# Probabilities times values in plain fp32 over four column groups of TensorE, in an attention and MLP kernel

## The chip, the cores and the metric

The kernel runs on one core of a Trainium2 chip. The metric is the device time of one execution in microseconds (us), the median over the runs. The engines are named as in the profile: PE is TensorE's matmul, PEld its weight loads, DVE is VectorE, ACT is ScalarE, POOL is GpSimd, SP is SyncE, which only issues DMAs here.

## The reference

The input is one sequence of 2048 tokens with 1024 features, all in fp32. It is normalized, passes an attention of 32 heads with 32 features each and is added to itself; then it is normalized twice and passes an MLP with 3584 hidden features. The attention works in four segments of 512 tokens. Within a segment it is plain causal softmax attention, and a memory of the earlier segments is mixed in by a gate:

```python
for s in range(N):                                     # N = 4 segments, L = 512 tokens
    logits = jnp.einsum("bhqd,bhkd->bhqk", qs, ks) * scale + mask
    p = _softmax(logits, axis=-1)
    a_dot = jnp.einsum("bhqk,bhkd->bhqd", p, vs)       # the product that is changed
    pq = phi(qs)
    num = jnp.einsum("bhld,bhde->bhle", pq, M)
    den = jnp.einsum("bhld,bhd->bhl", pq, z)[..., None] + 1e-6
    outs.append(g * num / den + (1.0 - g) * a_dot)
    M, z = M + jnp.einsum("bhld,bhle->bhde", phi(ks), vs), z + jnp.einsum("bhld->bhd", phi(ks))
h = x + o @ wo                                         # o: the heads' outputs side by side
h2 = h + mlp(_layernorm(h))                            # normalizes once more, then w1, gelu, w2
```

## The kernel before, in words

PE multiplies rounded operands (type fp32r) in one pass over the columns. To keep fp32's precision the kernel splits an operand in an upper half (the rounded value) and a lower half (what the rounding left) and adds up products of halves; three matmuls make a projection (`mm3`, lines 116 to 118).

The kernel treats the sequence in two halves of 1024 tokens. For each half it runs the attention, then the product with wo, then the MLP. In the attention the outer loop goes over eight groups of four heads and the inner one over the half's two segments. `dense` makes the projections of one group and segment (tiles kps, qps, vps) and prepares the values; `heads` treats the four heads of the group and segment before it, and `interleave` alternates the two, so that PE always has projections between the steps of a head. At the end of a half the last heads are interleaved with the first products with wo (tile pwo).

A head is a softmax over 512 keys, in four blocks of 128 keys (`jk`), causal: block `jk` is seen by queries from `128*jk` on, so it has 512, 384, 256 or 128 query columns. `qk` makes the logits (tile pqk), DVE adds the mask and takes the maximum, ACT takes the exponential into tile pr (`soft`, line 552). `ptr` transposes the probabilities on PE into tile ppt (in PSUM, two buffers) in three portions: n = 0 is block 0, n = 1 the blocks 1 and 3, n = 2 block 2. ACT copies each portion into pth, the upper half, and DVE subtracts into ptl, the lower half (`sub`, line 600).

`av` multiplies with the values, in two steps: n = 0 for the blocks 0 and 1, n = 1 for 3 and 2. The weights are a tile vs with 64 columns for each block and head: 32 columns are the values' upper half, 32 their lower half. Each block is multiplied with pth and with ptl, and all eight matmuls add up in one PSUM tile po with 64 partitions (one buffer, tag `av`). Between them `one_small` puts small matmuls of the memory (tiles pm and pmm). Then ACT copies partitions 32 to 63 of po into the head's rows of the tile ot, and `av_out` adds partitions 0 to 31 on DVE (line 624).

The order of the steps is written out: `PLAN = ('q1 r S2', 'q0 a0', 'q2 t0 w a1', 'q3 s0 o', 't1', 's1 t2')`. A letter is a step (q: `qk`, t: `ptr`, s and S: `sub`, a: `av`, o: `av_out`, r: `inverse`, w: `weigh`), the digit its argument, and between two entries the projections go on. a, o and S belong to the head before the one that t and s treat, and that is the head before the one of q. So `av_out` of one head stands two entries before the end of its slot, and a0 of the next head, which writes the one buffer of po again, in the second entry of the next slot. A scheduler of the framework then sets the final order on each engine's queue, by its own estimates; each queue runs in order.

Of the kernel before, what the change touches and what calls it, by code (L numbers as in the profile page):

```python
# [10 lines left out]
F32 = mybir.dt.float32  # L11
F32R = mybir.dt.float32r
AF = mybir.ActivationFunctionType
ALU = mybir.AluOpType
# [3 lines left out]
P = 128  # L18
# [21 lines left out]
def raw(ap):  # L40
    return ap.bitcast(F32)


def build(tc, x, wq, wk, wv, wo, beta, w1, b1, w2, b2, out):
    nc = tc.nc
# [3 lines left out]
    psum = top.enter_context(tc.tile_pool(name="psum", bufs=1, space=PSUM))  # L49

    def ps_dense(name):
        return psum.tile([P, 512], F32, tag="d", name=name, bufs=3)
# [33 lines left out]
    acts = {}  # L86
# [258 lines left out]
    def attention(half, first):  # L345
        ab, mask = acts["ab"], acts["mask"]
# [3 lines left out]
        def tmp(name):  # L350
            return ab.tile([P, 512], F32, tag="tmp", name=name, bufs=5)
# [34 lines left out]
        def one_small():  # L386
            if small:
                small.pop(0)()
# [16 lines left out]
        def dense(g, sl, ws, u):  # L405
# [58 lines left out]
            nc.scalar.copy(vt, vps)  # L464
            vs = ab.tile([P, 16, 64], F32R, name="vs", bufs=2)
            u["vs"] = vs
            omt = u["omt"] = tmp("omt") if s > 0 else None

            def late():
                vn = ps_dense("vn")  # L470
                for c in range(4):
                    nc.tensor.transpose(vn[:, c * P:(c + 1) * P], vt[:, c * P:(c + 1) * P], ident)
                vn3 = vn.rearrange("p (a b) -> p a b", b=DH)
                nc.scalar.copy(vs[:, :, 0:32], vn3)
                nc.vector.tensor_tensor(vs[:, :, 32:64], vn3, raw(vs[:, :, 0:32]), op=ALU.subtract)
                yield
                if s > 0:
                    om = tmp("om")

                    def memory(i2, ps):  # L480
                        pm = ps.rearrange("p (a b) -> p a b", a=2)
                        rg = ab.tile([P, 2, 32], F32, name="rg", bufs=2)[:, :, 0:4]
                        nc.vector.scalar_tensor_tensor(
                            rg, pm[:, :, 128:132], DEN_EPS, bb[:, 4 * g:4 * g + 4].unsqueeze(1).to_broadcast([P, 2, 4]),
                            op0=ALU.add, op1=ALU.mult)
                        nc.vector.reciprocal(rg, rg)
                        nc.vector.tensor_tensor(
                            om[:, i2 * 256:(i2 + 1) * 256].rearrange("p (a h e) -> p a h e", a=2, h=4),
                            pm[:, :, 0:128].rearrange("p a (h e) -> p a h e", h=4),
                            rg.unsqueeze(3).to_broadcast([P, 2, 4, DH]), op=ALU.mult)  # L490

                    for i2 in range(2):
                        smalls("pm", [(lambda ps, ii=ii: ps[:, 256 * ii:256 * ii + 132],
                                       pqh[:, (2 * i2 + ii) * P:(2 * i2 + ii + 1) * P],
                                       pql[:, (2 * i2 + ii) * P:(2 * i2 + ii + 1) * P], mzh, mzl, True, True)
                                      for ii in range(2)], partial(memory, i2))
                left = len(small)
                if s < 3:
                    def update(pmm):
                        nc.vector.tensor_tensor(MZ[:, g, 0:P], pmm[:, 0:P], MZ[:, g, 0:P], op=ALU.add)  # L500
                        own = MZ[:, g, 0:P].rearrange("p (h e) -> p h e", h=4)
                        nc.gpsimd.tensor_tensor(own, own, hsel.unsqueeze(2).to_broadcast([P, 4, DH]), op=ALU.mult)
                        z = ZC[:, g:g + 1]
                        nc.gpsimd.tensor_scalar(z, z, zc, None, op0=ALU.add)
                        nc.gpsimd.tensor_scalar(MZ[:, g, 128:132], hsel, z, None, op0=ALU.mult)

                    smalls("pmm", [(lambda ps: ps[:, 0:P].rearrange("p (a b) -> p a b", a=4),
                                    pkh[:, c * P:(c + 1) * P], pkl[:, c * P:(c + 1) * P],
                                    vs[:, 4 * c:4 * c + 4, 0:32], vs[:, 4 * c:4 * c + 4, 32:64], c == 0, c == 3)
                                   for c in range(4)], update)  # L510
                total = len(small)
                while len(small) > total - left:
                    yield
                yield
                if s > 0:
                    pom = ps_dense("pom")
                    for i in range(4):
                        one_small()
                        nc.tensor.transpose(pom[:, i * P:(i + 1) * P], om[:, i * P:(i + 1) * P], ident)
                    if s == 3:  # L520
                        yield
                        while acts["pth"][0] < 2:
                            yield
                    op = nc.scalar.copy(omt, pom)
                    if s == 3:
                        tc.add_manual_dep(op.ins, acts["pth"][1].ins.name, NOSYNC, reason="program order")
                while small:
                    yield
# [5 lines left out]
        koff = [0, 512, 1024, 896]  # L534
# [45 lines left out]
        def ptr(st, n):  # L580
            grp = ((0,), (1, 3), (2,))[n]
            if n == 0:
                st["pth"] = ab.tile([P, 1280], F32R, name="pth", bufs=2)
                st["ptl"] = ab.tile([P, 1280], F32R, name="ptl", bufs=2)
            pr, pth, ptl = st["pr"], st["pth"], st["ptl"]
            ppt = psum.tile([P, 512], F32, tag="pt", name="ppt", bufs=2)
            base = koff[grp[0]]
            w = 0
            for jk in grp:
                for i in range(jk, 4):  # L590
                    one_small()
                    o = koff[jk] - base + (i - jk) * P
                    nc.tensor.transpose(ppt[:, o:o + P], pr[:, offs[i] + jk * P:offs[i] + (jk + 1) * P], ident)  # L593
                    w += P
            acts["pth"] = n, nc.scalar.copy(pth[:, base:base + w], ppt[:, :w])  # L595
            st["sub", n] = (ptl[:, base:base + w], ppt[:, :w], raw(pth[:, base:base + w]))

        def sub(st, n):
            o, x0, x1 = st["sub", n]
            nc.vector.tensor_tensor(o, x0, x1, op=ALU.subtract)  # L600

        def av(st, n):
            u, j = st["u"], st["j"]
            if n == 0:
                st["po"] = psum.tile([P, 512], F32, tag="av", name="po", bufs=1)[0:64, :]
            po = st["po"]
            for jk in (0, 1) if n == 0 else (3, 2):
                w = 512 - P * jk
                v = u["vs"][:, 4 * jk + j, :]
                for part in ("pth", "ptl"):  # L610
                    if (jk, part) != (3, "ptl"):
                        one_small()
                    nc.tensor.matmul(po[:, P * jk:], v, st[part][:, koff[jk]:koff[jk] + w],  # L613
                                     start=(jk, part) == (0, "pth"), stop=(jk, part) == (2, "ptl"))
            if n == 1:
                if j == 0:
                    u["ot"] = ab.tile([P, 512], F32, name="ot", bufs=1)
                nc.scalar.copy(u["ot"][32 * j:32 * j + 32, :], po[32:64, :])

        def av_out(st):  # L620
            u, j, po = st["u"], st["j"], st["po"]
            ot = u["ot"]
            b = slice(32 * j, 32 * j + 32)
            nc.vector.tensor_tensor(ot[b, :], po[0:32, :], ot[b, :], op=ALU.add)
            if j == 3:
                w = u["w"]
                nc.gpsimd.tensor_tensor(w, ot, w, op=ALU.mult)
                if u["omt"] is not None:
                    nc.gpsimd.tensor_tensor(w, w, u["omt"], op=ALU.add)
                if u["g"] < NG - 1:  # L630
                    nc.sync.dma_start(o_dram[u["s"]][u["g"]], w)
                else:
                    oh, ol = o_tiles(half, u["s"] % 2)
                    split(None, w, oh[:, NG - 1, :], ol[:, NG - 1, :], hi_eng="scalar", lo_eng="vector")
# [35 lines left out]
        for g in range(NG):  # L670
            for sl in range(2):
                u = {"g": g, "s": 2 * half + sl}
# [24 lines left out]
    def o_tiles(half, sl):  # L697
        if ("o", half, sl) not in acts:
            acts["o", half, sl] = seg_tiles(sl, "o")
        return acts["o", half, sl]  # L700
# [626 lines left out]
    for half in range(2):  # L1327
# [5 lines left out]
        ab = acts["ab"]  # L1333
# [132 lines left out]
```

## Time and profile before

| | |
|---|---|
| median of 3 runs | 2314.42 us (2314.29 to 2317.33) |
| span of the profiled execution, first to last instruction | 2309.1 us |
| PE busy | 2273.1 us, 98% of the span, 11801 matmuls |
| DVE, ACT, POOL busy | 1519.7, 1227.7, 830.6 us |
| L600, 384 subtractions on DVE | 227.3 us, 600 ns each |
| L613, 1024 matmuls on PE, sum of their durations | 154.1 + 156.0 us |

The profile tells for each instruction its engine, its line, the tiles it writes and reads, when it starts and how long it takes. Matmuls are pipelined: the next one starts before the last one ends, so their durations add up to more than the time they take from PE; the distance from start to start tells that. "x512" after a group counts its instructions; "idle before" is the time that the engine stood still ahead of them, with what ended it. The span was taken from one execution; the median of the runs lies 5.3 us above it.

### The profile page before, as it was taken

How to read it: one execution, taken by the hardware profiler on the slowest of the kernel's cores; microseconds unless marked ns; L12 is line 12 of the kernel's file. 1: busy time of each engine (PE TensorE's matmuls, PEld its weight loads, DVE VectorE, ACT ScalarE, POOL GpSimd, SP SyncE). 2: the span in 40 equal slices, each digit the busy share in tenths (PEclk: the TensorE clock that was granted, in tenths of full speed). 3: DMA queues.
4: the chain of work that ended last, by engine and by line, in shares of the span. 5: the costliest groups of instructions: out<-in, count | busy, mean ns of one | idle time of the engine just before them, and what ended most of it. 6: DMA issues, size and time to landing. Idle time of an engine off the chain costs nothing.

```text
span 2309.1 us, 34959 instructions
## 1 busy us (share of the span) xinstructions
PE 2273.1 (98%) x11801; PEld 1895.7 (82%) x11801; DVE 1519.7 (66%) x3045; ACT 1227.7 (53%) x2581; POOL 830.6 (36%) x686
## 2 busy tenths in 40 slices
PE   8999999999999999999999998999999999999999
PEld 6888888877888887888888886788888888888887
DVE  6777777776655565777777776574566766566663
ACT  6777777774453445777777775363344223332221
POOL 4222222224244442233232224244445654155430
PEclk9999999999999999999999999999999999999999
DMA  6333343344466654433333343466567976476772
GB/s 187 104 95 97 98 102 95 94 140 164 138 209 173 186 166 138 120 100 95 95 95 99 95 118 119 160 202 195 156 190 265 348 249 217 152 259 218 249 235 92
DMA packets 329885, 364.00 MB, mean 158 GB/s; under 512 B 28750, under 2 KB 221802, under 8 KB 329706
## 3 DMA queue, kind: packets, MB, share of 16 engines
q1 hardware_dynamic: 266538, 325.06, 46.5%
q10 hardware_dynamic: 63168, 36.71, 5.3%
q8 instruction: 93, 1.52, 0.3%
q14 instruction: 86, 0.70, 0.1%
HBM read 234.98 MB, written 76.35 MB: 135 GB/s over the span
## 4 chain that ended last, share of the span: by engine, by line
PE 69%; DMA 1%; POOL 1%; ACT 1%; DVE 1%; issue 1%; SPq 0%; POOLq 0%; ACTq 0%; DVEq 0%
PE po L1300 23%; PE bps L904 10%; PE cps L904 7%; PE dps L904 6%; PE po L613 3%; PE ppt L593 3%; PE pqk L543 2%; PE vps L116 1%; PE vps L117 1%; PE vps L118 1%; PE kps L116 1%; PE kps L117 1%; PE qps L117 1%; PE qps L116 1%; PE kps L118 1%; PE qps L118 1%
## 5 line engine op out<-in xcount | busy, mean ns | idle before, releaser
L552 ACT ACTIVATE pr<-pr,mx 128x256 f32<-128x256 f32 (+3 forms) x512 | 287.1, 561 | 163.5 <-DVE mx L544 154.7
L544 DVE CUSTOM_DVE_ANT_0 pr<-pqk,mask 128x256 f32<-128x256 f32 (+3 forms) x512 | 244.5, 486 | 107.1 <-PE pqk L543 105.9
L600 DVE TENSOR_TENSOR ptl<-ppt,pth 128x512 fp32r<-128x512 f32 (+1 forms) x384 | 227.3, 600 | 94.9 <-ACT pth L595 92.4
L593 PE MATMUL ppt<-ident,pr 128*128 128x128 f32 x1280 | 223.1, 277 | 1.0 <-DVE ptl L600 0.8
L595 ACT CAST pth<-ppt 128x512 fp32r<-128x512 f32 (+1 forms) x384 | 194.0, 517 | 40.2 <-PE ppt L593 33.1
L93 POOL TENSOR_TENSOR wl<-wr,wh 128x1024 fp32r<-128x1024 f32 x52 | 124.8, 2399 | 229.5 <-PE pqk L543 128.0
L1310 DVE TENSOR_TENSOR c<-c,po 128x512 f32<-128x512 f32 x160 | 105.4, 683 | 149.6 <-PE po L1300 146.7
L593 PEld LDWEIGHTS ppt<-ident,pr 128*128 128x128 f32 x1280 | 165.0, 141 | 30.8 <-DVE ptl L600 1.9
L543 PE MATMUL pqk<-ks,qs 96*128 96x256 f32 (+3 forms) x512 | 161.6, 316 | 0.0
L613 PE MATMUL po<-ptl,vs 128*64 128x512 f32 (+3 forms) x512 | 154.1, 310 | 4.3 <-DVE ptl L600 4.1
L613 PE MATMUL po<-pth,vs 128*64 128x512 f32 (+3 forms) x512 | 156.0, 327 | 0.0
L1300 PE MATMUL po<-w2h,zh 128*128 128x512 f32 x378 | 120.8, 389 | 0.0
L543 PEld LDWEIGHTS pqk<-ks,qs 96*128 96x128 f32 x512 | 96.5, 189 | 21.6 <-issue 0.2
L904 PE MATMUL bps<-zh,sb 128*128 128x512 f32 x336 | 111.1, 391 | 0.0
L904 PE MATMUL bps<-zh,sa 128*128 128x512 f32 x336 | 110.8, 390 | 0.0
L1157 POOL TENSOR_TENSOR w2r<-w2r 128x512 f32<-128x512 f32 x54 | 85.5, 1595 | 70.2 <-DMA w2r<-in_B_w 63.6
L116 PE MATMUL vps<-yh,wh 128*128 128x512 f32 x256 | 109.4, 427 | 0.9 <-DVE MZ L500 0.9
L116 PE MATMUL kps<-yh,wh 128*128 128x512 f32 (+1 forms) x264 | 110.0, 417 | 0.0
L116 PE MATMUL qps<-yh,wh 128*128 128x512 f32 x256 | 106.9, 418 | 0.0
L1300 PE MATMUL po<-w2h,hl 128*128 128x512 f32 x322 | 103.0, 390 | 0.0
L117 PE MATMUL kps<-yl,wh 128*128 128x512 f32 (+1 forms) x264 | 102.3, 388 | 0.1
L118 PE MATMUL kps<-yh,wl 128*128 128x512 f32 (+1 forms) x264 | 101.9, 386 | 0.0
(253 smaller groups left out, 6548.4 us busy)
## 6 DMA issues: line engine op xcount, KB each, us to landing
hr<-h_dram SPq DMA_DIRECT2D x112, 448.0 KB, 5.7
w2r<-in_B_w SPq DMA_DIRECT2D x122, 256.0 KB, 4.1
r<-in_B_w SPq DMA_DIRECT2D x56, 512.0 KB, 4.8
h_dram<-ht ACTq DMA_DIRECT2D x84, 256.0 KB, 3.8
ks<-kh SPq DMA_DIRECT2D x256, 64.0 KB, 2.0
qs<-qh SPq DMA_DIRECT2D x256, 64.0 KB, 2.0
wr<-in_A_wo SPq DMA_DIRECT2D x32, 512.0 KB, 4.5
wx<-in_B_w SPq DMA_DIRECT2D x56, 256.0 KB, 3.6
```

Of the source, the lines that this page charges most:

```text
L116: nc.tensor.matmul(ps, ah, bh, start=first, stop=False)
L117: nc.tensor.matmul(ps, ah, bl, start=False, stop=False)
L118: acts["mm"] = nc.tensor.matmul(ps, al, bh, start=False, stop=last)
L543: nc.tensor.matmul(pqk[:, :n], u["qs"][j][:, i * P:(i + 1) * P], u["ks"][j][:, 0:n], start=True, stop=True)
L544: nc.vector.tensor_tensor_reduce(out=st["pr"][:, offs[i]:offs[i] + n], in0=pqk[:, :n], in1=mask[:, 512 - n:512], op0=ALU.add, op1=ALU.min, ...
L552: nc.scalar.activation(pi, pi, AF.Exp, bias=mx[:, i:i + 1], scale=-1.0, accum_out=mx[:, 4 + i:5 + i])
L593: nc.tensor.transpose(ppt[:, o:o + P], pr[:, offs[i] + jk * P:offs[i] + (jk + 1) * P], ident)
L595: acts["pth"] = n, nc.scalar.copy(pth[:, base:base + w], ppt[:, :w])
L600: nc.vector.tensor_tensor(o, x0, x1, op=ALU.subtract)
L613: nc.tensor.matmul(po[:, P * jk:], v, st[part][:, koff[jk]:koff[jk] + w], start=(jk, part) == (0, "pth"), stop=(jk, part) == (2, "ptl"))
L904: nc.tensor.matmul(ps, x_[:, c, :], y_[:, c, :], start=first and c == 0 and n == 0, stop=last and c == 3 and n == 2, skip_group_check=True)
L1300: nc.tensor.matmul(ps, x_[:, k], y_[k], start=opens and k == 0 and i == 0, stop=closes and k == self.KP - 1 and i == 2, skip_group_check=True)
```

## The change

The probabilities are no longer split: ACT copies ppt into one tile pt in plain fp32, and the subtraction on DVE goes. `late` in `dense` makes one more copy of the transposed values on ACT, vf, in plain fp32 (vs stays, the memory's product uses it). `av` has four matmuls of plain fp32 operands in place of eight of rounded ones. Their weights are 32 columns of vf, and block `jk` uses column group `jk` of PE (`tile_position=(0, 32 * jk)`), so that its sum stands in partitions `32*jk` to `32*jk + 31` of po. The small matmuls that stood between the eight now stand ahead of the first. ACT copies the first group into ot, and DVE adds the other three, over 384, 256 and 128 columns.

```diff
+            vf = u["vf"] = ab.tile([P, 16, 32], F32, name="vf", bufs=2)
...
                 nc.scalar.copy(vs[:, :, 0:32], vn3)
+                nc.scalar.copy(vf, vn3)
...
         def ptr(st, n):
             if n == 0:
-                st["pth"] = ab.tile([P, 1280], F32R, name="pth", bufs=2)
-                st["ptl"] = ab.tile([P, 1280], F32R, name="ptl", bufs=2)
+                st["pt"] = ab.tile([P, 1280], F32, name="pt", bufs=2)
...
-            acts["pth"] = n, nc.scalar.copy(pth[:, base:base + w], ppt[:, :w])
-            st["sub", n] = (ptl[:, base:base + w], ppt[:, :w], raw(pth[:, base:base + w]))
+            acts["pth"] = n, nc.scalar.copy(pt[:, base:base + w], ppt[:, :w])
...
         def av(st, n):
-                st["po"] = psum.tile([P, 512], F32, tag="av", name="po", bufs=1)[0:64, :]
+                st["po"] = psum.tile([P, 512], F32, tag="av", name="po", bufs=1)
-            for jk in (0, 1) if n == 0 else (3, 2):
+            for _ in range(4 if n == 0 else 3):
+                one_small()
+            for jk in (0, 1) if n == 0 else (2, 3):
                 w = 512 - P * jk
-                v = u["vs"][:, 4 * jk + j, :]
-                for part in ("pth", "ptl"):
-                    if (jk, part) != (3, "ptl"):
-                        one_small()
-                    nc.tensor.matmul(po[:, P * jk:], v, st[part][:, koff[jk]:koff[jk] + w],
-                                     start=(jk, part) == (0, "pth"), stop=(jk, part) == (2, "ptl"))
+                b = slice(32 * jk, 32 * jk + 32)
+                nc.tensor.matmul(po[b, P * jk:], u["vf"][:, 4 * jk + j, :], st["pt"][:, koff[jk]:koff[jk] + w],
+                                 start=True, stop=True, tile_position=(0, 32 * jk), skip_group_check=True)
...
-                nc.scalar.copy(u["ot"][32 * j:32 * j + 32, :], po[32:64, :])
+                nc.scalar.copy(u["ot"][32 * j:32 * j + 32, :], po[0:32, :])
...
         def av_out(st):
-            nc.vector.tensor_tensor(ot[b, :], po[0:32, :], ot[b, :], op=ALU.add)
+            for k in (1, 2, 3):
+                c = slice(P * k, 512)
+                nc.vector.tensor_tensor(ot[b, c], po[32 * k:32 * k + 32, c], ot[b, c], op=ALU.add)
```

On PE's queue, at the step a0 of a head of the second segment (L398 are the small products, L543 or L545 the logits, L116 the next projection), before:

```order
L543 MATMUL pqk<-ks,qs 128x128 [waits DVE_49]
L398 MATMUL pm<-mzh,pqh 128x132 [waits Activation_49]
L613 MATMUL po<-pth,vs 64x512 [waits DVE_49]
L398 MATMUL pm<-mzl,pqh 128x132
L613 MATMUL po<-ptl,vs 64x512
L398 MATMUL pm<-mzh,pql 128x132
L613 MATMUL po<-pth,vs 64x384 [waits Activation_49]
L398 MATMUL pm<-mzh,pqh 128x132
L613 MATMUL po<-ptl,vs 64x384 [waits DVE_49]
L116 MATMUL qps<-yh_194,wh 128x512 [waits DVE_49,PE_49]
```

and with the change:

```order
L545 MATMUL pqk<-ks,qs 128x128 [waits DVE_49]
L398 MATMUL pm<-mzh,pqh 128x132 [waits Activation_49]
L398 MATMUL pm<-mzl,pqh 128x132
L398 MATMUL pm<-mzh,pql 128x132
L398 MATMUL pm<-mzh,pqh 128x132
L611 MATMUL po<-pt,vf 32x512 [waits DVE_49,Activation_49]
L611 MATMUL po<-pt,vf 32x384 [waits Activation_49]
L116 MATMUL qps<-yh_194,wh 128x512 [waits DVE_49,PE_49]
```

The two matmuls of the step stand side by side behind the small ones, and wait for ACT's copies alone and, the first of them, for DVE's last add of the head before.

On DVE's queue, from the logits of one slot's fourth query block to those of the next slot's first (L544 or L546 is the mask and maximum, the reciprocal is that of the softmax sums), before:

```order
L544 ISA pr,mx<-pqk,mask 128x512 [waits PE_49]
L544 ISA mx 128x1
L624 TENSOR_TENSOR ot<-po,ot 32x512 [waits Activation_49]
L431 TENSOR_TENSOR ql<-qps,qh 128x512 [waits DMAHW6_49,Activation_49]
L559 RECIPROCAL rs<-mx 128x4 [waits Activation_49]
L600 TENSOR_TENSOR ptl<-ppt,pth 128x512 [waits Activation_49]
L460 TENSOR_TENSOR pkl<-pkn,pkh 128x512 [waits Activation_49]
```

and with the change:

```order
L546 ISA pr,mx<-pqk,mask 128x512 [waits PE_49]
L546 ISA mx 128x1
L624 TENSOR_TENSOR ot<-po,ot 32x384 [waits Activation_49]
L431 TENSOR_TENSOR ql<-qps,qh 128x512 [waits DMAHW6_49,Activation_49]
L624 TENSOR_TENSOR ot<-po,ot 32x256 [waits DVE_49]
L561 RECIPROCAL rs<-mx 128x4 [waits Activation_49]
L624 TENSOR_TENSOR ot<-po,ot 32x128 [waits DVE_49]
L460 TENSOR_TENSOR pkl<-pkn,pkh 128x512 [waits Activation_49]
```

The subtraction is gone, and the three adds, each of which waits for the one before it, are spread among other work; the last of them stands behind the reciprocal, which waits for ACT's exponential.

More of the change, by code (lines that the diff above doesn't have):

```diff
@@ L582, in ptr @@
             if n == 0:
-                st["pth"] = ab.tile([P, 1280], F32R, name="pth", bufs=2)
-                st["ptl"] = ab.tile([P, 1280], F32R, name="ptl", bufs=2)
-            pr, pth, ptl = st["pr"], st["pth"], st["ptl"]
+                st["pt"] = ab.tile([P, 1280], F32, name="pt", bufs=2)
+            pr, pt = st["pr"], st["pt"]
             ppt = psum.tile([P, 512], F32, tag="pt", name="ppt", bufs=2)
@@ L594, in ptr @@
                     w += P
-            acts["pth"] = n, nc.scalar.copy(pth[:, base:base + w], ppt[:, :w])
-            st["sub", n] = (ptl[:, base:base + w], ppt[:, :w], raw(pth[:, base:base + w]))
+            acts["pth"] = n, nc.scalar.copy(pt[:, base:base + w], ppt[:, :w])
         def sub(st, n):
-            o, x0, x1 = st["sub", n]
-            nc.vector.tensor_tensor(o, x0, x1, op=ALU.subtract)
+            pass
         def av(st, n):
```

## The prediction

> **What bounds the kernel now.** I read the busy line of the page first, then a table of stretches, then TensorE's (PE's) waits, then the order of time inside one head.
>
> ```profile
> span 2309.1 us, 34959 instructions
> PE 2273.1 (98%) x11801; PEld 1895.7 (82%) x11801; DVE 1519.7 (66%) x3045; ACT 1227.7 (53%) x2581; POOL 830.6 (36%) x686
> ```
>
> The columns of the table are start:end, length, then busy time and instructions of PE, its weight loads, DVE, ACT and POOL, and the granted clock. The rows are the two attention stretches, where all edited lines run, and the two tails in which the last heads meet the first output products.
>
> ```profile
> 58.00:500.00 442.00, 439.73 (x2689) 372.79 (x2688) 323.52 (x916) 323.98 (x832) 114.72 (x122) 1.00 0.39 100
> 500.00:545.00 45.00, 40.43 (x228) 33.00 (x227) 32.08 (x79) 29.78 (x70) 10.96 (x10) 0.96 0.29 98
> 935.00:1380.00 445.00, 442.44 (x2709) 375.35 (x2709) 328.33 (x943) 330.55 (x844) 132.96 (x133) 1.00 0.38 100
> 1380.00:1440.00 60.00, 52.45 (x277) 42.03 (x276) 40.01 (x88) 35.73 (x78) 21.74 (x15) 0.97 0.39 128
> ```
>
> In the attention stretches PE is busy 439.73 of 442 us and 442.44 of 445 at full clock, while DVE and ACT are busy 73% of the time. PE's work sets the pace there, and an engine beside it can give back only what PE spends waiting for it. Of PE's waits the first two of these are for the probabilities' lower halves, the third is the only one ahead of a small product:
>
> ```profile
> PE po L613 <- DVE ptl L600: 4.1, 3, 1.5
> ...
> PE ppt L593 <- DVE ptl L600: 0.8, 1, 0.8
> PE pmm L398 <- DVE kl L417: 0.6, 1, 0.6
> ```
>
> The first two are 4.9 us in the whole span (total, times, longest). Here is one head's probabilities times values on PE (start, duration, instruction):
>
> ```profile
> 502.08 0.39 PE L118 MATMUL pwo<-wh,ol 128*128 128x512 f32 x1
> 502.31 0.22 PE L543 MATMUL pqk<-ks,qs 96*128 96x128 f32 x1
> 502.37 0.39 PE L613 MATMUL po<-pth,vs 128*64 128x512 f32 x1
> 502.60 0.40 PE L613 MATMUL po<-ptl,vs 128*64 128x512 f32 x1
> 502.83 0.33 PE L613 MATMUL po<-pth,vs 128*64 128x384 f32 x1
> 503.01 0.33 PE L613 MATMUL po<-ptl,vs 128*64 128x384 f32 x1
> 503.18 0.40 PE L116 MATMUL pwo<-wh,oh 128*128 128x512 f32 x1
> ...
> 504.06 0.60 PE L593 MATMUL ppt<-ident,pr 128*128 128x128 f32 x4
> 504.42 0.30 PE L613 MATMUL po<-pth,vs 128*64 128x128 f32 x1
> 504.56 0.23 PE L613 MATMUL po<-ptl,vs 128*64 128x128 f32 x1
> 504.62 0.28 PE L613 MATMUL po<-pth,vs 128*64 128x256 f32 x1
> 504.74 0.28 PE L613 MATMUL po<-ptl,vs 128*64 128x256 f32 x1
> 504.85 0.40 PE L116 MATMUL pwo<-wh,oh 128*128 128x512 f32 x1
> ```
>
> Durations overlap, so what an instruction costs PE is the distance to the next start: 0.23 us for 512 columns (502.37 to 502.60), 0.06 for 128 (502.31 to 502.37), that is 0.443 ns a column. All these count as one pass per column.
>
> **The change part by part.**
>
> *Removed from PE:* eight matmuls a head. The first four take 502.37 to 503.18, 0.81 us. The last four take 504.42 to 504.85, but the transposes ahead still hold the array at their start. Four of them span 0.60 us and, by the row below, one lasts 0.277, so their starts lie (0.60 - 0.277)/3 = 0.11 us apart, and the fourth gives the array up at about 504.50. That leaves 0.35 us. Together 1.16 us a head.
>
> ```profile
> L593 PE MATMUL ppt<-ident,pr 128*128 128x128 f32 x1280 | 223.1, 277 | 1.0 <-DVE ptl L600 0.8
> ```
>
> *Added to PE:* four plain fp32 matmuls a head, over 512, 384, 256 and 128 columns. In the compiled program each is two loads of weights and two matmuls over the same columns (before and after hold 11801 PE matmuls alike), so 2560 columns a head stream as before. What a column costs in such a pass no row shows. Lower bound: the price of the rounded operands, 0.443 ns. Upper bound: the only rows whose operands are both plain f32, the transposes, at 0.11 us for 128 columns, 0.86 ns. The transposes' 0.11 is not their weight load: the matmul after them at 504.42 has a load of half the width, and yet it lasts 0.30 instead of its twin's 0.23. I take 0.86, the row of the same operands.
>
> What the column groups save no row shows either. One after another the passes cost 2560 x 0.86 = 2.20 us a head. If PE takes instructions in order and a pass runs beside its predecessor when their column groups differ, then at each of the two places the second pass of the first block runs beside the first pass of the second block, and the shorter is hidden: 512 + 384 + 384 columns are left at the first place, 256 + 128 + 128 at the second, 1792 together, 1.54 us. Were both passes of the second block hidden, 2 x (512 + 256) = 1536 columns would be left, 1.32 us. I take the staggered case, between the two ends: the two passes of one block load different weights into the same group and must follow each other, while neighbouring blocks share neither weights nor output columns.
>
> The Trainium skill, TensorE: Matmul & The Clock Gate, section Part 3: Packing small matmuls, says that matmuls in different column tiles run at the same time, and gives 2.38 times for three tiles of 512 columns. No row of this trace has two column groups, so none agrees or disagrees; by that rule the four passes of a place would cost hardly more than the longest block, as in the side-by-side case, and without it the sum is the 2.20 us.
>
> Per head 1.54 - 1.16 = +0.38 us, times 128 heads = +49 us on PE. With PE busy as in the table, nothing covers it.
>
> *Small products* (the pm and pmm matmuls) that stood between the eight now stand ahead of the first: the same count, no cost while their operands are there; their one wait in the trace is 0.6 us, so I put the move at 0, between -0.6 (the wait goes) and +2 us (three more like it).
>
> *DVE and ACT:*
>
> ```profile
> L600 DVE TENSOR_TENSOR ptl<-ppt,pth 128x512 fp32r<-128x512 f32 x256 | 176.8, 691 | 93.4 <-ACT pth L595 92.1
> L600 DVE TENSOR_TENSOR ptl<-ppt,pth 128x256 fp32r<-128x256 f32 x128 | 53.4, 417 | 1.5 <-ACT pth L595 0.3
> L624 DVE TENSOR_TENSOR ot<-po,ot 32x512 f32<-32x512 f32 x128 | 87.0, 680 | 3.9 <-ACT ot L618 0.9
> L544 DVE CUSTOM_DVE_ANT_0 pr<-pqk,mask 128x384 f32<-128x384 f32 x128 | 71.2, 556 | 94.2 <-PE pqk L543 94.2
> L544 DVE CUSTOM_DVE_ANT_0 pr<-pqk,mask 128x128 f32<-128x128 f32 x128 | 36.5, 285 | 0.6 <-PE pqk L543 0.5
> L474 ACT CAST vs<-vn 128x512 fp32r<-128x512 f32 x32 | 18.8, 586 | 26.7 <-PE vn L472 26.6
> ```
>
> The 384 subtractions go: 176.8 + 53.4 = 230 us of DVE. One add of 0.680 becomes three, of 384, 256 and 128 columns, by the rows of like width (32 or 128 partitions make no difference: 0.680 beside 0.691 for 512 columns) 0.556 + 0.417 + 0.285 = 1.26 us: +0.58 x 128 = +74 us. DVE loses 156 us. Since PE waited 4.9 us for the removed results, that is what the relief is worth: -5 us (bounds -5 and 0, as the copy of ACT, which PE now waits for, comes 0.7 us before the subtraction ended). ACT gains 32 copies of v at 0.586 = 19 us over two stretches in which it idles a quarter: 0, covered by PE's longer time; uncovered it would be at most 19. The copy of the probabilities is the same size in another type, and the copy of the first group into ot the same width.
>
> The three adds are a new wait: the first block of the next head writes the same bank (one buffer), so it is queued behind the last add, and dense matmuls behind it.
>
> ```profile
> 303.84 0.58 ACT L618 COPY ot<-po 32x512 f32<-32x512 f32 x1
> 305.06 0.67 DVE L624 TENSOR_TENSOR ot<-po,ot 32x512 f32<-32x512 f32 x1
> 306.26 0.15 DVE L559 RECIPROCAL rs<-mx 128x4 f32<-128x4 f32 x1
> 306.50 0.69 DVE L600 TENSOR_TENSOR ptl<-ppt,pth 128x512 fp32r<-128x512 f32 x1
> 307.71 0.39 PE L613 MATMUL po<-pth,vs 128*64 128x512 f32 x1
> ```
>
> One add ended at 305.73, and the next head's first matmul started at 307.71. Where the last add stands behind the reciprocal (306.41 here) it ends near 306.7; 1 us is left, and the subtraction at 306.50 is gone. So 0, and if the cover goes, each 0.1 us of lateness costs 128 x 0.1 = 13 us.
>
> *Sum:* 2309.1 + 49 - 5 = 2353 us of span. The median of the runs shown, 2314.42, lies 5.3 above that span, so 2358 us for the median.
>
> **The rivals.**
>
> No overlap: the second group waits for the first. For it: PE's rows of one column group follow each other strictly; against: disjoint columns share neither weights nor output. 2.20 - 1.16 = +1.04 us, x 128 = +133, -5: 2442 us.
>
> Whole overlap of the two blocks of a place: 1.32 - 1.16 = +0.16, x 128 = +20, -5: 2329 us. Against it: the second pass of the first block stands ahead of the second block's first in the queue.
>
> A change of the group width empties the array. A matmul of 512 columns lasts 0.39 and the next starts after 0.23, so 0.16 us lost at each of four changes a head: +82 us on the forecast, 2440. Against it: at 502.31 to 502.37 and at 503.01 to 503.18 the present program enters and leaves 64-column weights at the plain pace. The Trainium skill, TensorEngine Tiling (Array Packing), section Key Properties, states that a change of tiling mode drains TensorE; those rows show no drain, so the rule gets a small chance, that of positions other than zero.
>
> Not slower: a plain fp32 pass streams at the rounded pace, 0.443 ns a column. Then the staggered count costs 1792 x 0.443 = 0.79 us, -0.37 x 128 = -47, -5: 2262 us. It decides below 1.16/1792 = 0.65 ns a column. For it: the count of columns is unchanged; against: the transposes' 0.86.
>
> Late adds: PE waits at every head, 0.3 us on top: +38, 2396 us.
>
> **How the numbers follow.** Staggered overlap 0.42, whole overlap 0.13, no overlap 0.28, drain 0.05, late adds 0.04, not slower 0.08. The predicted time is that of the first, 2358. The range goes from 2325, a little under whole overlap, to 2455, a little over no overlap, and so takes in both ends of what the column groups save; left out are the not-slower case and sums beyond no overlap. A measurement of this kernel can tell 0.2%, 4.6 us, from no change. Faster by more than that: 0.07. Within it: 0.03. Slower: 0.90.
>
> **What the changed profile would show.** The four fp32 matmuls in pairs of rows, 1024 in all; the distance from the first start to the next dense matmul 1.1 us at the first place and 0.44 at the second (0.9 and 0.44 with whole overlap, 1.54 and 0.66 without any; half of these if a pass runs at the rounded pace). Starts of the second pass of block 0 and the first of block 1 nearly equal would show the overlap. DVE busy near 1364 us, ACT near 1247, PE still 97% or more, and the two attention stretches longer by about 22 us each, with everything after 1440 us only shifted. The prediction is wrong if a plain fp32 column costs far from 0.86 ns, or if PE waits for the adds or the copies in the middle of a stretch.

## The result

The change makes the kernel slower: 2401.41 us median (2400.83 to 2403.32, 4 runs) against 2315.47 (2314.29 to 2317.33, 4 runs) in the same sessions, a ratio of 1.0376 with a 95% interval of 1.0361 to 1.0391 (the two medians alone divide to 1.0371, inside it). That is +86 us; the forecast was 2358, +44, within a range of 2325 to 2455. The sign and the range held, the size is twice the forecast.

The page after, its span and busy line:

```profile
span 2398.9 us, 34973 instructions
PE 2375.4 (99%) x11801; PEld 1829.8 (76%) x11801; DVE 1416.3 (59%) x2917; ACT 1235.9 (52%) x2613; POOL 821.1 (34%) x686
```

PE is busy 99% of the span, 98% before, and its busy time grew by 102 us, so the 89.8 us of longer span are longer work of PE. (The medians differ by 86; the span before is from an execution some 3 us quicker than the median.) DVE lost 103 us of busy time, and the span shows no gain from it. By durations it lost 155, as worked out (the subtractions' 230 went, the adds grew from 87.0 to 162.2 us); its records overlap where they stand close, and busy time counts such an overlap once, so less of it went. PE's waits (total, times, longest) hold none for the probabilities or the adds any more; these are the longest:

```profile
PE pt L269 <- ACT xt L259: 10.0, 2, 8.7
PE pwo L117 <- POOL zl L93: 5.2, 2, 3.3
PE pwo L117 <- POOL wl L93: 1.5, 2, 1.2
PE pt L150 <- DVE yl L154: 0.8, 1, 0.8
PE pom L521 <- DVE om L489: 0.6, 2, 0.5
```

Here is one head after, its two places on PE in order of time; the four fp32 matmuls of a place (two for each block) are merged into one row:

```profile
299.97 0.39 PE L118 MATMUL vps<-yh,wl 128*128 128x512 f32 x1
300.20 0.22 PE L545 MATMUL pqk<-ks,qs 96*128 96x128 f32 x1
300.35 1.05 PE L611 MATMUL po<-pt,vf 128*32 128x512 f32 x4
301.33 0.50 PE L116 MATMUL vps<-yh,wh 128*128 128x512 f32 x1
301.67 0.40 PE L117 MATMUL vps<-yl,wh 128*128 128x512 f32 x1
...
302.31 0.60 PE L594 MATMUL ppt<-ident,pr 128*128 128x128 f32 x4
302.84 0.62 PE L611 MATMUL po<-pt,vf 128*32 128x256 f32 x4
303.39 0.50 PE L116 MATMUL vps<-yh,wh 128*128 128x512 f32 x1
303.72 0.40 PE L117 MATMUL vps<-yl,wh 128*128 128x512 f32 x1
```

The last of the first place's four, from a narrower window of the same view:

```profile
300.81 0.59 PE L611 MATMUL po<-pt,vf 128*32 128x512 f32 x1
```

Read by distances from start to start, as in the prediction, a place has three parts.

- *Streaming.* 300.35 to 301.33 is 0.98 us at the first place, 302.84 to 303.39 is 0.55 at the second. Block 0's two passes start 0.454 us apart (300.35 to 300.81, by the unrounded starts), 0.886 ns a column; a second pass as long ends at 301.26, and 0.07 us are left until the next matmul starts (0.09, if the second pass takes the 0.429 us that it takes with one group, below). The whole-overlap case said 0.88 and 0.44, the staggered one 1.10 and 0.44.
- *Entering.* Behind the logits of 128 columns the first matmul started 0.06 us later in the kernel before; now it starts 0.15 later (300.20 to 300.35). Behind the fourth transpose (started at 302.31 + 3 x 0.11 = 302.64, holding the array to 302.75) it starts at 302.84. Each time 0.09 us too late.
- *Leaving.* The dense matmul behind the next one comes 0.34 and 0.33 us later than that one, in place of 0.23: another 0.10 each.

The group by form for 300.36 to 300.70 shows what runs in the first part of the place (the rows before L611 have only their modelled ends there):

```profile
L611 PE MATMUL po<-pt,vf 128*32 128x512 f32 x1 | 0.6, 617 | 0.0
L611 PE MATMUL po<-pt,vf 128*32 128x384 f32 x1 | 0.5, 510 | 0.0
```

A matmul over 512 columns and one over 384 run together from the start: that is block 0 and block 1, side by side, although the second matmul of block 0 stands between them in the program (the run with one group, below, shows that order). It is so at the first place of 126 of the 128 heads. The weight loads tell what entering and leaving is:

```profile
299.98 0.19 PEld L545 LDWEIGHTS pqk<-ks,qs 96*128 96x128 f32 x1
300.35 0.14 PEld L611 LDWEIGHTS po<-pt,vf 128*32 128x32 f32 x4 [0.19 <-issue]
301.33 0.19 PEld L116 LDWEIGHTS vps<-yh,wh 128*128 128x128 f32 x1 [0.83 <-issue]
301.44 0.19 PEld L117 LDWEIGHTS vps<-yl,wh 128*128 128x128 f32 x1
```

The same queue before, at the place that the prediction showed:

```profile
502.08 0.19 PEld L543 LDWEIGHTS pqk<-ks,qs 96*128 96x128 f32 x1
502.31 0.14 PEld L613 LDWEIGHTS po<-pth,vs 128*64 128x64 f32 x1
502.37 0.14 PEld L613 LDWEIGHTS po<-ptl,vs 128*64 128x64 f32 x1
```

Before, the load for the matmul of 502.37 started at 502.31, under the matmul ahead of it. After, the loads start only when the first matmul does (300.35), and the load of the next dense matmul starts only at 301.33, when that matmul starts, with 0.83 us of idle loading behind it. No load runs ahead into the column groups or out of them.

### The profile page after: what moved, and what is told of

It is laid out like the page before. It is cut to its first block, busy times and chain, and to the rows that moved or that the text cites. A ratio compares the mean times of both kernels' runs of the same rounds, so it can differ in the third digit from the quotient of the medians.

```text
span 2398.9 us, 34973 instructions
## 1 busy us (share of the span) xinstructions
PE 2375.4 (99%) x11801; PEld 1829.8 (76%) x11801; DVE 1416.3 (59%) x2917; ACT 1235.9 (52%) x2613; POOL 821.1 (34%) x686
## 4 chain that ended last, share of the span: by engine, by line
PE 91%; POOL 3%; DMA 2%; ACT 1%; DVE 1%; issue 1%; SPq 1%; POOLq 0%; ACTq 0%
PE po L1300 21%; PE bps L904 9%; PE po L611 8%; PE cps L904 6%; PE dps L904 6%; PE ppt L594 6%; PE qps L116 3%; PE pqk L545 3%; PE vps L116 3%; PE kps L116 3%; PE vps L117 2%; PE vps L118 2%; PE qps L117 2%; PE qps L118 2%; PE kps L117 2%; PE kps L118 2%
## 5 line engine op out<-in xcount | busy, mean ns | idle before, releaser
L546 DVE CUSTOM_DVE_ANT_0 pr<-pqk,mask 128x256 f32<-128x256 f32 (+3 forms) x512 | 249.5, 490 | 348.3 <-PE pqk L545 343.7
L596 ACT COPY pt<-ppt 128x512 f32<-128x512 f32 (+1 forms) x384 | 195.3, 512 | 115.0 <-PE ppt L594 114.4
L611 PE MATMUL po<-pt,vf 128*32 128x512 f32 (+3 forms) x1024 | 215.1, 445 | 0.0
L624 DVE TENSOR_TENSOR ot<-po,ot 32x384 f32<-32x384 f32 (+2 forms) x384 | 162.2, 422 | 33.3 <-ACT ot L616 21.4
L545 PE MATMUL pqk<-ks,qs 96*128 96x256 f32 (+3 forms) x512 | 161.4, 316 | 0.0
L116 PE MATMUL qps<-yh,wh 128*128 128x512 f32 x256 | 119.0, 465 | 0.0
L116 PE MATMUL kps<-yh,wh 128*128 128x512 f32 (+1 forms) x264 | 116.1, 440 | 0.0
L116 PE MATMUL vps<-yh,wh 128*128 128x512 f32 x256 | 115.4, 451 | 0.0
L545 PEld LDWEIGHTS pqk<-ks,qs 96*128 96x128 f32 x512 | 96.2, 188 | 22.7 <-issue 1.2
L116 PEld LDWEIGHTS qps<-yh,wh 128*128 128x128 f32 x256 | 48.3, 189 | 75.0 <-issue 71.8
```

The costliest lines, as they stand in the source:

```text
L116: nc.tensor.matmul(ps, ah, bh, start=first, stop=False)
L545: nc.tensor.matmul(pqk[:, :n], u["qs"][j][:, i * P:(i + 1) * P], u["ks"][j][:, 0:n], start=True, stop=True)
L546: nc.vector.tensor_tensor_reduce(out=st["pr"][:, offs[i]:offs[i] + n], in0=pqk[:, :n], in1=mask[:, 512 - n:512], op0=ALU.add, op1=ALU.min, ...
L596: acts["pth"] = n, nc.scalar.copy(pt[:, base:base + w], ppt[:, :w])
L611: nc.tensor.matmul(po[b, P * jk:], u["vf"][:, 4 * jk + j, :], st["pt"][:, koff[jk]:koff[jk] + w], start=True, stop=True, tile_position=(0, ...
L624: nc.vector.tensor_tensor(ot[b, c], po[32 * k:32 * k + 32, c], ot[b, c], op=ALU.add)
```

## The experiments

From this I formed theory 1: whole overlap, 0.886 ns a column and pass, and 0.26 us for entering and leaving at each place (0.09 of entering, the 0.07 behind the streaming, 0.10 of leaving). Its rivals were a plain column price without overlap, and overlap with a high column price and no cost of switching.

**All blocks in one column group.** This separates overlap from the price of a column.

```diff
-                nc.tensor.matmul(po[b, P * jk:], u["vf"][:, 4 * jk + j, :], st["pt"][:, koff[jk]:koff[jk] + w],
-                                 start=True, stop=True, tile_position=(0, 32 * jk), skip_group_check=True)
+                nc.tensor.matmul(po[0:32, P * jk:], u["vf"][:, 4 * jk + j, :], st["pt"][:, koff[jk]:koff[jk] + w],
+                                 start=jk == 0, stop=jk == 3, tile_position=(0, 0), skip_group_check=True)
...
-            for k in (1, 2, 3):
-                c = slice(P * k, 512)
-                nc.vector.tensor_tensor(ot[b, c], po[32 * k:32 * k + 32, c], ot[b, c], op=ALU.add)
```

> The change with all four blocks in column group 0, so that they add up in PSUM and the three DVE adds go; nothing else differs. Theory 1 (read from the trace after: the two blocks of a place stream wholly side by side at 0.886 ns a column and pass, and each of the two places pays about 0.26 us for entering and leaving the column groups): nothing runs side by side any more, so a head costs 2560 x 0.886 + 2 x 0.26 = 2.79 us in place of 1.88, +0.91 x 128 = +116 us: about 2518 us. Theory 2 (no overlap; a plain fp32 column simply costs 1.88/2560 = 0.73 ns): the time stays at 2401. Theory 3 (whole overlap and no cost of switching; a column costs 1.88/1536 = 1.22 ns): 2560 x 1.22 = 3.13 us a head, 2401 + 160 = 2561 us.

Measured: 2508.97 us, ratio to the kernel before 1.0835 (1.0818 to 1.0852). Theory 1 said 2518; both rivals are out, by over 100 and by 50 us. The place in its timeline takes 1.62 us from the first matmul to the next dense one, against 0.98 with groups:

```profile
305.32 1.69 PE L610 MATMUL po<-pt,vf 128*32 128x512 f32 x4
306.94 0.50 PE L116 MATMUL qps<-yh,wh 128*128 128x512 f32 x1
307.27 0.39 PE L117 MATMUL qps<-yl,wh 128*128 128x512 f32 x1
```

The third start comes 0.33 us after the second here too: leaving costs the same without overlap. From narrower windows, the place's four matmuls in two rows:

```profile
305.32 1.04 PE L610 MATMUL po<-pt,vf 128*32 128x512 f32 x2
306.20 0.81 PE L610 MATMUL po<-pt,vf 128*32 128x384 f32 x2
```

Within one group the two passes of block 0 run first, then the two of block 1. By the unrounded starts block 0's first pass takes 0.453 us and its second 0.429, 0.84 ns a column. So the 0.886 above, read from a first pass, holds some 0.02 us of entering. The column groups' overlap was worth 2508.97 - 2401.41 = 108 us (the three adds that went as well were no row of PE's waits).

**Full width.** The same products and count of passes, with weights over all 128 columns: no group is entered or left.

```diff
-                b = slice(32 * jk, 32 * jk + 32)
-                nc.tensor.matmul(po[b, P * jk:], u["vf"][:, 4 * jk + j, :], st["pt"][:, koff[jk]:koff[jk] + w],
-                                 start=True, stop=True, tile_position=(0, 32 * jk), skip_group_check=True)
+                v = u["vf"][:, 4 * jk:4 * jk + 4, :].rearrange("p a b -> p (a b)")
+                nc.tensor.matmul(po[:, P * jk:], v, st["pt"][:, koff[jk]:koff[jk] + w],
+                                 start=jk == 0, stop=jk == 3, skip_group_check=True)
...
-                nc.scalar.copy(u["ot"][32 * j:32 * j + 32, :], po[0:32, :])
+                nc.scalar.copy(u["ot"][32 * j:32 * j + 32, :], po[32 * j:32 * j + 32, :])
```

The adds of `av_out` go as above.

> The change with weights of 128 columns (the values of all four heads of the group, of which only the head's own 32 rows of the result are used) over the whole array, so that there are neither column groups nor overlap; the four blocks add up in PSUM and the DVE adds go. Theory 1: 2560 x 0.886 = 2.27 us a head and no switching, against 1.88: +0.39 x 128 = +50, about 2451 us, some 67 below the kernel with all blocks in one group, which is the price of the two places' switching. Theory 2: 2401. Theory 3: 2561, the same as with one group.

Measured: 2438.09 us, ratio 1.0529 (1.0515 to 1.0544). It is 71 us below the kernel with one group (2508.97), which over 256 places is 0.28 us a place; theory 1 said 67. It lies 13 below the 2451 expected, since theory 1 had both its terms a little off. By the rows a head takes 2.21 us here (1.56 at the first place, read below, and 0.65 at the second by the same reading), in place of 2.27, and 1.91 with the change, in place of 1.88; the 0.09 us between come to 12 over 128 heads. The first place:

```profile
307.94 0.22 PE L545 MATMUL pqk<-ks,qs 96*128 96x128 f32 x1
308.00 1.72 PE L611 MATMUL po<-pt,vf 128*128 128x512 f32 x4
309.26 0.68 PE L116 MATMUL vps<-yh,wh 128*128 128x512 f32 x1
309.79 0.39 PE L117 MATMUL vps<-yl,wh 128*128 128x512 f32 x1
```

The fp32 matmuls start 0.06 us behind the logits here, as the rounded ones did before. The place takes 308.00 to 309.79, less the dense matmul's own 0.23, that is 1.56 us for 1792 columns, 0.87 ns each. That holds 0.05 us of a bare load in the first pass (0.48 us by the unrounded starts); the second pass takes 0.429 us, as with one group.

**One place.** All four blocks at a1, so that the groups are entered once a head.

```diff
-            for jk in (0, 1) if n == 0 else (2, 3):
+            for jk in () if n == 0 else (0, 1, 2, 3):
```

> The change with all four blocks at the second place (a1) and none at the first, so that the column groups are entered and left once a head. Theory 1: the 512 columns of block 0 hide the other three, 1024 x 0.886 = 0.91 us, and one switch, 0.26: 1.17 us a head in place of 1.88, -0.71 x 128 = -91 us: about 2310 us, the time of the kernel before. Theory 2 (no overlap): 2401. Theory 3 (overlap, 1.22 ns a column, no switching): 1024 x 1.22 = 1.25 us, about 2320.

Measured: 2325.29 us, ratio 1.0045 (1.0032 to 1.0059). 76 us of the 86 are gone. All eight matmuls of a head take as long as two over 512 columns did, so four groups run side by side as two did:

```profile
303.95 1.04 PE L611 MATMUL po<-pt,vf 128*32 128x512 f32 x8
304.92 0.50 PE L116 MATMUL qps<-yh,wh 128*128 128x512 f32 x1
305.26 0.40 PE L117 MATMUL qps<-yl,wh 128*128 128x512 f32 x1
```

It stays 15 us above theory 1. Part of it stands in PE's waits, in two rows that neither the kernel before nor the change has:

```profile
PE pmm L398 <- ACT r L367: 6.4, 7, 0.9
...
PE pqk L545 <- DVE mx L546: 1.6, 7, 0.2
```

The rest, some 7 us, I did not trace. Theory 3's 2320 lies nearer, but the two runs above rule that theory out.

**The kernel before without the subtraction.** What is DVE's relief worth alone?

```diff
-            o, x0, x1 = st["sub", n]
-            nc.vector.tensor_tensor(o, x0, x1, op=ALU.subtract)
+            pass
...
-                    nc.tensor.matmul(po[:, P * jk:], v, st[part][:, koff[jk]:koff[jk] + w],
+                    nc.tensor.matmul(po[:, P * jk:], v, st["pth"][:, koff[jk]:koff[jk] + w],
```

> The kernel before without the subtraction on DVE: the second matmul of each block uses the upper half again, so the lower half of the probabilities is left out of the sum, and PE's work is unchanged. It measures what the relief of DVE alone (230 us of its busy time) is worth. The prediction: PE no longer waits for the lower halves, -5 us, 2310 us. Rival: nothing, 2315, since another wait takes the place; or much more, -20 us or beyond, if DVE's queue held PE up in ways that PE's waits don't show.

Measured: 2311.75 us against 2314.9, ratio 0.9986 (0.9977 to 0.9994): -3 us for 230 us of DVE's time. In place of the 4.9 us PE's waits there have two new rows, one for a small product and one for the copy ahead of the removed subtraction:

```profile
PE pmm L398 <- ACT r L367: 3.0, 7, 0.5
...
PE po L610 <- ACT pth L594: 2.0, 2, 1.1
```

**The small products ahead.** The kernel before with only the small matmuls moved as the change moves them.

```diff
+            for _ in range(4 if n == 0 else 3):
+                one_small()
             for jk in (0, 1) if n == 0 else (3, 2):
...
-                    if (jk, part) != (3, "ptl"):
-                        one_small()
```

> The kernel before with one edit: the small products of the memory that stood between the eight matmuls of a head stand ahead of the first, as in the change. The prediction put this move at 0 (-0.6 to +2 us). What the trace after suggests: a small product behind another costs about 0.11 us, as long as its load of 128 columns of weights, and one ahead of a matmul with narrow weights 0.06 to 0.09; 149 of them stand behind another now, and PE's time at the small products went from 64 to 74 us: +8 us, 2323.

Measured: 2317.17 us against 2313.87, ratio 1.0014 (1.0006 to 1.0023): +3 us. The prediction's 0, with +2 as its bound, was a little low, and the 8 too high. From start to next start the small products take 64.1 us in the kernel before, 69.5 here and 74.2 in the change, while the matmuls of the probabilities and their transposes take 2.2 less here. Some 4 us of the change's 74.2 are the entering of the groups: at 45 places a small product stands last ahead of them, and the next start comes 0.20 us after it in place of 0.11.

**Balanced.** All at one place, and the columns spread so that each group streams 320 in place of up to 512.

```diff
-            for jk in (0, 1) if n == 0 else (2, 3):
-                w = 512 - P * jk
-                b = slice(32 * jk, 32 * jk + 32)
-                nc.tensor.matmul(po[b, P * jk:], u["vf"][:, 4 * jk + j, :], st["pt"][:, koff[jk]:koff[jk] + w],
-                                 start=True, stop=True, tile_position=(0, 32 * jk), skip_group_check=True)
+            parts = ((0, 0, 0, 320), (1, 1, 128, 448), (2, 2, 256, 512), (3, 0, 320, 512), (2, 1, 448, 512), (3, 3, 384, 512))
+            for i, (k, jk, c0, c1) in enumerate(parts if n == 1 else ()):
+                o = koff[jk] - P * jk
+                nc.tensor.matmul(po[32 * k:32 * k + 32, c0:c1], u["vf"][:, 4 * jk + j, :], st["pt"][:, o + c0:o + c1],
+                                 start=i < 4, stop=i != 2 and i != 3, tile_position=(0, 32 * k), skip_group_check=True)
...
+                nc.scalar.copy(u["ot"][32 * j:32 * j + 32, 0:320], po[0:32, 0:320])
+                nc.scalar.copy(u["ot"][32 * j:32 * j + 32, 320:512], po[96:128, 320:512])
...
+            for k, c in ((1, slice(128, 448)), (2, slice(256, 512))):
```

> The change with all of a head's columns at the second place (a1), and block 0's last 192 and block 1's last 64 columns moved to the column groups of the blocks 3 and 2, where they add up in PSUM, so that each group streams 320 columns; ACT copies the result of two groups, DVE adds two in place of three. Theory 1 (whole overlap, 0.886 ns a column and pass, 0.26 us for a switch): 640 x 0.886 + 0.26 = 0.83 us a head where the kernel before needs 1.16: -0.33 x 128 = -42, the small products ahead +8, no waits for the subtraction -3: about 2278 us, faster than both kernels. Theory 3 (1.22 ns a column, no switching), already against the runs with one group and with full width, would give 0.78 us a head and 2271, hardly another time. Where overlap needed whole blocks (two matmuls of one head that add up in a group stop the others), it would stay near 2325, as with whole blocks at one place.

Measured: 2287.85 us against 2313.87, ratio 0.9891 (0.9876 to 0.9906): 26 us faster than the kernel before and 114 faster than the change.

```profile
300.20 0.75 PE L611 MATMUL po<-pt,vf 128*32 128x320 f32 x12
300.88 0.50 PE L116 MATMUL qps<-yh,wh 128*128 128x512 f32 x1
...
PE pmm L398 <- ACT r L367: 6.4, 7, 0.9
PE pqk L545 <- DVE mx L546: 4.0, 17, 0.8
```

A head's products take 300.20 to 300.88, 0.68 us, with 0.09 and 0.10 around them 0.87 in place of 1.16. That is -37 us; the two waits of PE below it (from its waits, in total; neither the kernel before nor the change has them) give 10 back, and that is the distance to the 2278 expected. Two matmuls that add up in one group did not stop the other groups.

## Why the prediction was right in sign and wrong in size

*The bound.* Right: PE sets the pace, and its added work lengthened the span by 89.8 us.

*The price of a plain fp32 column.* Right: 0.86 was taken from the transposes, 0.84 is what a second pass shows with one group and with full width, with two passes for each matmul.

*What the column groups save.* The staggered case was taken, whole overlap came (its chance was 0.13). The reason I gave, that a block's second pass stands ahead of the next block's first in the queue, does not hold PE back: block 1's first pass starts with block 0's. In the sum this term was too high by 2358 - 2329 = 29 us. The Trainium skill, TensorE: Matmul & The Clock Gate, section Part 3: Packing small matmuls, had this side: tiles in different columns run together, and the rows of the two places and of the eight matmuls at one place agree.

*Entering and leaving the groups.* This is the step that failed. I put the drain aside because the program "enters and leaves 64-column weights at the plain pace". Those rows were no evidence: in its source the kernel before names a column group (`tile_position`) for no matmul, and the change for its fp32 matmuls alone. So narrow weights were there, a change of groups was not. Narrow weights in plain fp32 don't cost it either. That shows at a place of the kernel after where a transpose with 16 columns of weights and no column group (tile pw) stands ahead, first in the loads, then in the matmuls:

```profile
71.90 0.09 PEld L574 LDWEIGHTS pw<-ident,rs 128*16 128x16 f32 x1
72.21 0.14 PEld L611 LDWEIGHTS po<-pt,vf 128*32 128x32 f32 x4 [0.22 <-issue]
```

```profile
72.01 0.27 PE L574 MATMUL pw<-ident,rs 128*16 128x128 f32 x1
72.21 0.40 PE L611 MATMUL po<-pt,vf 128*32 128x256 f32 x2
```

The load for 72.01 ran ahead, 0.11 us before its matmul. The load of the groups did not, and the first matmul in the groups started 0.20 us after 72.01, where with full width it starts 0.11 after a transpose. Measured: 71 us between one group and full width, 0.28 us a place, where the rival said 0.16 at each of four changes, 0.32 a place and 82 us. Its mechanism is what the rows show, though not all of it is the emptied array: the 0.10 of each leaving is a load that could not run ahead. The Trainium skill, TensorEngine Tiling (Array Packing), section Key Properties, has a drain at a change of tiling mode; the 0.09 us at each entry and the load that starts only behind the last matmul agree.

*DVE, the adds and ACT.* -5 us was -3 (0.9986). The adds' wait, put at 0, is no row of PE's waits, and neither are ACT's 32 copies.

*The small products.* Put at 0 with a bound of +2, measured +3.

Put together with measured terms: from the rows a head after costs 0.98 + 0.55 of streaming, 2 x 0.09 of entering and 2 x 0.10 of leaving, 1.91 us, against 1.16; +0.75 x 128 = +96, -3 for DVE, +3 for the small products: +96 us, where the spans differ by 89.8. PE's waits sum to 30.3 us before and 19.1 after; 4.9 of the difference were for the subtractions, and the other 6 would cover what the sum is too high. The two errors of the prediction, -29 and +71, are of opposite sign (2358 - 29 + 71 = 2400 against 2401.41). That the range held is luck: its upper end was drawn for groups that don't overlap, and it took in the cost of entering and leaving only because they overlap better than was taken.

## What to carry to other kernels

Price a change of TensorE's column groups as its own term, here about 0.28 us for going in and out, and count how often it happens: the same products cost 2401 us with two places a head, 2325 with one, and 2288 with one place and evenly filled groups. Before a row is taken as evidence that a cost isn't there, see that it really contains the thing that would cost: 64-column weights looked like a smaller tile, but named no column group. An engine that is busy two thirds of the time, with 230 us taken off it, gave 3 us, since the bound engine had waited 5 us for it.

## What was not expected of the hardware

TensorE started a matmul of another column group ahead of an earlier one in the program: the first matmul of the second block starts with the first of the first block (the two rows for 300.36 to 300.70), with four groups as with two. So the sentence ahead of the prediction that each queue runs in order doesn't hold for PE once matmuls name different column groups. And none of its weight loads runs ahead across the border between matmuls that name no column group and matmuls that name one: 0.28 us for each stay, with overlap or without.
